# Centring block 0 and multiplying its tokens' scale onto the first layer's sums in an FNet-plus-MLP kernel

## The chip, the cores and the metric

The kernel runs on one core of a Trainium2 chip. The core has a matrix engine (PE, with its weight loads as PEld), a vector engine (DVE), an activation engine (ACT), a general engine (POOL) and a queue processor (SP); SP and POOL issue the transfers here. Every engine works off its own instructions in order and waits for the others by semaphores. The metric is the time of one execution in microseconds (us); runs are given by their median.

## What is computed

```python
x  = A_x                                     # 1 x 2048 x 640, float32
xn = (x - mean(x)) / sqrt(var(x) + 1e-5)     # over the 640 columns
a, b = xn @ dft_hid_re.T, xn @ dft_hid_im.T
y = dft_seq_re @ a - dft_seq_im @ b          # Fourier mixing, real part
h = gelu_tanh(xn @ w1 + b1)                  # w1: 640 x 1536
out = x + y + h @ w2 + b2                    # w2: 1536 x 640
```

## The kernel before, in words

The 2048 tokens are four blocks of 512; a block is four row tiles of 128 tokens by 640 columns. Each float32 operand of a product is split into a high part (ACT copies it to the matrix format, `high`, L186) and a low part (DVE subtracts, `low`, L189), and a product is three matmuls of 512 columns: high by high, high by low, low by high.

The program is written in the order in which every engine is to work; no scheduler moves anything. It begins with block 0. Its four row tiles are loaded (L208) and normalized (L686 to L727: statistics on DVE and ACT, a square root on ACT, three steps of DVE that refine the reciprocal, then subtraction and scaling), while PE runs `NWARM` matmuls on zeros (L666). PE turns the normalized tiles by 20 transposes of 128x128 (L682) into five PSUM banks, from which `XT[j]`, the high and low parts of the five column chunks, are split.

Then come the 12 hidden units of block 0, 128 columns of `w1` each. `hidden(g)` (L308) is 15 matmuls (L320) into one of three banks. `unit` (L332) applies bias and gelu on ACT, from the bank into `ab`; `split_unit` (L343) makes the high and low parts `hs`. `output(g)` (L363) is 15 matmuls (L300 to L302) onto five banks that sum over the units. Step `i` of the loop at L1157 prepares `w1` of unit i+3 and `w2` of unit i+1 (a high part on ACT and a low part on DVE each), issues loads of later weights (three buffers for each of `w1r` and `w2r`), does work of other blocks in `background(i)`, runs `hidden(i+2)`, the gelu and split of that unit, `late(i)`, and `output(i)`.

The other blocks need normalized rows too, for the Fourier part (`xn` in DRAM, written by `put_rows`) and for the hidden units of blocks 1 and 2. Rows of tiles 8 to 11 ("b") and 4 to 7 ("a") are loaded, get statistics (`ln_stats`, L210: two passes over half a row tile and a merge) in steps 0 to 2, a scale (`ln_scale`, L218) and are normalized on DVE (`ln_apply`, L229): "b" in `late(1)`, "a" at the start of step 3. `put_z` (L758) then moves them on the chip into a form `Z`, "b" by eight transfers on SP and eight on POOL, "a" by 16 on POOL. `make_forms` in steps 4, 6 and 7 turns columns of `Z` on DVE (L259) and splits them; `add` (L463) forms differences.

All loads of weights stand on SP's queue in program order. In step 1 the loads of `w1` for unit 7 and of `w2` for unit 5 stand ahead of the eight `z_b` transfers; the load of `w1` for unit 8 stands behind them. A load of `w1` into a buffer waits until the low part of the unit that had it is done.

Of the kernel before, what the change touches and what calls it, by code (L numbers as in the profile page):

```python
# [10 lines left out]
F32 = mybir.dt.float32  # L11
# [4 lines left out]
P = 128  # L16
# [3 lines left out]
NWARM = 19  # L20
NGATE = (7, 10)
# [5 lines left out]
def kernel(  # L27
# [88 lines left out]
    def bank(k):  # L116
        return banks[:, k]
# [15 lines left out]
    ident = early.tile([P, P], F32, name="ident")  # L133
    es_r = ExitStack()
# [41 lines left out]
    def split(hi, lo, src, perm=False):  # L176
# [6 lines left out]
        low(l, s, h)  # L183
# [26 lines left out]
    def ln_stats(c):  # L210
        m = MV
        st = ST[c % 2]
        half = D // 2
        for h in range(2):
            nc.vector.bn_stats(st[:, h, :], xt[c][:, h * half : (h + 1) * half])  # L215
        nc.vector.bn_aggr(m[:, slot[c], 0:2], st.rearrange("p a b -> p (a b)"))  # L216

    def ln_scale(n):  # L218

        m = MV[:, :n]  # L220
        ve, r, t = m[:, :, 2], m[:, :, 3], m[:, :, 4]
        nc.scalar.activation(r, m[:, :, 1], AF.Sqrt, bias=eps[:, 0:1])
        nc.vector.tensor_scalar(ve, m[:, :, 1], EPS, None, op0=ALU.add)
        nc.vector.reciprocal(r, r)
        nc.vector.scalar_tensor_tensor(t, r, -0.5, r, op0=ALU.mult, op1=ALU.mult)
        nc.vector.tensor_tensor(t, t, ve, op=ALU.mult)
        nc.vector.scalar_tensor_tensor(r, t, 1.5, r, op0=ALU.add, op1=ALU.mult)

    def ln_apply(c, eng=nc.vector):  # L229
        m = MV[:, slot[c]]  # L230
        eng.tensor_scalar(xt[c], xt[c], m[:, 0:1], m[:, 3:4], op0=ALU.subtract, op1=ALU.mult)

    def ln_apply_chunked(dst, c, j0=0, j1=ND):

        m = MV[:, slot[c]]
        nc.vector.tensor_scalar(
            chunked(dst)[:, :, j0:j1],
            xt[c].rearrange("p (q c i) -> p q c i", q=Q, i=B)[:, :, j0:j1],
            m[:, 0:1],
            m[:, 3:4],  # L240
            op0=ALU.subtract,
            op1=ALU.mult,
        )
# [43 lines left out]
    def prep_w1(i, n=None):  # L287
        if i < NF:
            W1[i] = slots[1, i]
            split(W1[i][:, 0], W1[i][:, 1], w1r.pop(i if n is None else n).rearrange("p a b -> p (a b)"))  # L290

    def prep_w2(i):
        if i < NF:
            W2[i] = slots[2, i]
            split(W2[i][:, 0], W2[i][:, 1], w2r.pop(i), perm=True)
# [36 lines left out]
    def unit(g, acc, plus=None, a=None):  # L332

        i = g % NF
        if a is None:
            a = mr.tile([P, TB], F32, tag="ab", bufs=2, name=f"ab{g}")
        if plus is not None:
            add(a, plus, acc)
            acc = a
        nc.scalar.activation(a, acc, AF.Gelu_apprx_tanh, bias=b1c[:, i : i + 1])  # L340
        return a
# [9 lines left out]
    FIRST = [(0, 0), (0, 2), (1, 0), (1, 2), (0, 1), (2, 0), (2, 2), (1, 1), (3, 0), (3, 2)]  # L351
    FIRST += [(2, 1), (4, 0), (4, 2), (3, 1), (4, 1)]

# [326 lines left out]
    def transpose_x(c, j0, j1):  # L680
# [5 lines left out]
    last = 1  # L686
    f, m = MV[:, 0], MV[:, last]
    root, step, shift = f[:, 3:4], f[:, 4:5], f[:, 5:6]
    ln_stats(0)
    nc.scalar.activation(root, f[:, 1:2], AF.Sqrt, bias=eps[:, 0:1])  # L690
    scratch = mr.tile([P, 2 * TB], F32, tag="hs", bufs=3, name="scratch")[:, :D]
    nc.scalar.activation(scratch, xt[last], AF.Copy, scale=-1.0 / D, accum_out=m[:, 5:6])
    nc.scalar.activation(
        chunked(xp[:, last]),
        xt[last].rearrange("p (q c i) -> p q c i", q=Q, i=B),
        AF.Identity,
        bias=m[:, 5:6],
    )
    nc.scalar.activation(scratch, xp[:, last], AF.Square, scale=D**-0.5, accum_out=m[:, 1:2])
    nc.vector.reciprocal(root, root)  # L700
    nc.vector.scalar_tensor_tensor(step, root, -0.5, root, op0=ALU.mult, op1=ALU.mult)
    nc.vector.scalar_tensor_tensor(step, f[:, 1:2], EPS, step, op0=ALU.add, op1=ALU.mult)
    for c in (2, 3):
        ln_stats(c)
    others = MV[:, 1:NC]
    v, r, t = others[:, :, 1], others[:, :, 3], others[:, :, 4]
    nc.scalar.activation(r, v, AF.Sqrt, bias=eps[:, 0:1])  # L707
    nc.vector.scalar_tensor_tensor(root, step, 1.5, root, op0=ALU.add, op1=ALU.mult)  # L708
    nc.vector.scalar_tensor_tensor(shift, f[:, 0:1], -1.0, root, op0=ALU.mult, op1=ALU.mult)
    nc.vector.reciprocal(r, r)  # L710
    nc.vector.scalar_tensor_tensor(t, r, -0.5, r, op0=ALU.mult, op1=ALU.mult)
    nc.vector.scalar_tensor_tensor(t, v, EPS, t, op0=ALU.add, op1=ALU.mult)
    nc.vector.scalar_tensor_tensor(r, t, 1.5, r, op0=ALU.add, op1=ALU.mult)
    nc.scalar.activation(  # L714
        chunked(xp[:, 0]),
        xt[0].rearrange("p (q c i) -> p q c i", q=Q, i=B),
        AF.Identity,
        bias=shift,
        scale=root,
    )  # L720
    nc.scalar.activation(xp[:, last], xp[:, last], AF.Copy, scale=m[:, 3:4])
    W1[0], first_w1 = slots[1, 0], w1r.pop(0).rearrange("p a b -> p (a b)")
    nc.scalar.activation(W1[0][:, 0], first_w1, AF.Copy)

    for j0, j1 in ((0, 2), (2, ND)):
        for c in (2, 3):
            ln_apply_chunked(xp[:, c], c, j0, j1)  # L727
# [6 lines left out]
    nc.vector.tensor_tensor(W1[0][:, 1], first_w1, W1[0][:, 0].bitcast(F32), op=ALU.subtract)  # L734
    for j in range(ND):
        split(XT[j][:, 0], XT[j][:, 1], tacc[j])
        if j == 0:
            hidden(0, slice(0, 1))
            transpose_x(3, ND - 1, ND)
    nc.scalar.activation(m[:, 0:1], m[:, 5:6], AF.Copy, scale=-1.0)  # L740
# [8 lines left out]
    acc0 = hidden(0, slice(1, None))  # L749
    prep_w1(1)  # L750
    acc1 = hidden(1)
    prep_w2(0)
    prep_w1(2)
# [19 lines left out]

    def background(i):

        if i == 0:
            for c in range(NC):
                ln_apply(c)
            put_rows(0, row_places)
            ln_stats(8)  # L780
            ln_stats(9)
        if i == 1:
            ln_stats(11)
        if i == 2:
            ln_stats(4)
            ln_stats(5)
# [4 lines left out]
        if i == 6:  # L791
# [3 lines left out]
        if i >= 6:  # L795
            (ua, va), (ub, vb) = ((Z[k][:, :, : 2 * B], Z[k][:, :, 2 * B : 4 * B]) for k in "ab")
        if i == 6:
            add(ub, ub, ua, ALU.subtract)
        if i == 7:
            make_forms("a", "oa0", "va1")  # L800
            open_place(*PLACES[8])
            make_forms("b", "t10", "t11")
        if i == 8:
            add(vb, vb, ub, ALU.subtract)
            turn_x("t20", "b")
            turn_x("t21", "b")
            add(ua, vb, ua, ALU.subtract)
            add(va, va, vb, ALU.subtract)
            load_xo(0)
            for q in range(Q):  # L810
                nc.sync.dma_start(
                    b2c[q * B : (q + 1) * B], b2[q * DQ : (q + 1) * DQ].rearrange("(c i) -> i c", i=B)
                )

    def late(i):

        if i == 0:
            ln_stats(10)
        if i == 1:
            ln_scale(NC)  # L820
            Z["b"] = zo_tile("z_b")
            for c in range(2 * NC, 3 * NC):
                ln_apply(c)
            put_z(Z["b"], A["rows_b"], nc.gpsimd, nc.sync)
            put_rows(2, A["rows_b"])
        if i == 2:
            ln_stats(6)
            ln_stats(7)

    def normalize_a():  # L830
        ln_scale(NC)
        Z["a"] = as_z(row_places)
        for c in range(NC, 2 * NC):
            ln_apply(c)
        put_z(Z["a"], A["rows_a"], nc.gpsimd)

# [250 lines left out]
    def between(p):  # L1087
# [10 lines left out]
        if p == 3:  # L1098
            ln_scale(NC)
# [55 lines left out]
    gelu(0, acc0)  # L1155
    gelu(1, acc1)
    for i in range(NF - 2):  # L1157
        prep_w1(i + 3)
        if i == 3:
            normalize_a()  # L1160
# [3 lines left out]
        prep_w2(i + 1)  # L1164
# [3 lines left out]
        background(i)  # L1168
        acc = hidden(i + 2)
        if i == NF - 3:  # L1170
            more_forms()
        gelu(i + 2, acc)
# [584 lines left out]
```

## Time and profile before

The median of three runs is 851.38 us (851.08 to 852.01).

| | profiled execution before |
|---|---|
| span, first to last instruction | 849.9 us; the page gives no other time of this execution |
| mean granted TensorE clock | 0.998 |
| PE busy | 841.9 us, 99% |
| DVE busy | 686.7 us, 81% |
| ACT busy | 368.6 us, 43% |
| POOL busy | 67.7 us, 8% |
| transfers | 166.53 MB, mean 196 GB/s |

The median of the runs is 1.5 us above this span. A row of the timeline has start, length, engine, line, operation, what is written and read, a count, and in brackets the idle time before it with what ended that. `xab`, `xc`, `as`, `r` and `rt` are the places where the split weights stand, `w1r` and `w2r` the weights as loaded, `banks` is PSUM. "SPq" is SP's queue of issues. A matmul row of 0.39 us has its latency in it; matmuls start 0.23 us apart.

### The profile page before, as it was taken

How to read it: one execution, taken by the hardware profiler on the slowest of the kernel's cores; microseconds unless marked ns; L12 is line 12 of the kernel's file. 1: busy time of each engine (PE TensorE's matmuls, PEld its weight loads, DVE VectorE, ACT ScalarE, POOL GpSimd, SP SyncE). 2: the span in 40 equal slices, each digit the busy share in tenths (PEclk: the TensorE clock that was granted, in tenths of full speed). 3: DMA queues.
4: the chain of work that ended last, by engine and by line, in shares of the span. 5: the costliest groups of instructions: out<-in, count | busy, mean ns of one | idle time of the engine just before them, and what ended most of it. 6: DMA issues, size and time to landing. Idle time of an engine off the chain costs nothing.

```text
span 849.9 us, 10599 instructions
## 1 busy us (share of the span) xinstructions
PE 841.9 (99%) x3711; PEld 696.7 (82%) x3711; DVE 686.7 (81%) x909; ACT 368.6 (43%) x527; POOL 67.7 (8%) x116
## 2 busy tenths in 40 slices
PE   8999999999999999999999999999999999999997
PEld 7888888888888888888888888888888888888886
DVE  7979889767844778979978887889967998885687
ACT  7655666654453555443444344232323433323241
POOL 0440024222301000000000000000000000000002
PEclk9999999999999999999999999999999999999999
DMA  8995667878977897958744679763745799705464
GB/s 230 288 248 158 139 163 250 260 223 305 262 192 199 333 323 138 209 120 193 158 137 107 167 220 283 165 144 99 214 150 156 229 237 234 303 19 180 124 172 108
DMA packets 199141, 166.53 MB, mean 196 GB/s; under 512 B 61648, under 2 KB 170192, under 8 KB 198576
## 3 DMA queue, kind: packets, MB, share of 16 engines
q1 hardware_dynamic: 188320, 140.42, 62.7%
q0 software_dynamic: 7600, 24.91, 8.7%
q10 hardware_dynamic: 3168, 0.52, 0.3%
q8 instruction: 29, 0.48, 0.2%
q14 instruction: 24, 0.20, 0.1%
HBM read 115.75 MB, written 46.14 MB: 190 GB/s over the span
## 4 chain that ended last, share of the span: by engine, by line
PE 98%; DMA 1%; DVE 0%; ACT 0%; SPq 0%; issue 0%; ACTq 0%
PE banks L301 29%; PE banks L302 29%; PE banks L300 29%; PE banks L320 10%; DMA row<-in_A_x_dram 1%; PE banks L682 0%; DVE st L215 0%; ACT xp L714 0%; SPq L208 0%; DVE yo L1722 0%; DVE mv L216 0%; ACT mv L707 0%; DVE mv L708 0%; ACTq L707 0%
## 5 line engine op out<-in xcount | busy, mean ns | idle before, releaser
L186 ACT ACTIVATE as<-r 128x1024 fp32r<-128x1024 f32 x80 | 85.0, 1062 | 171.1 <-PE banks L302 150.4
L300 PE MATMUL banks<-as,xab 128*128 128x512 f32 x407 | 158.3, 389 | 0.0
L302 PE MATMUL banks<-as,xab 128*128 128x512 f32 x407 | 158.3, 389 | 0.0
L301 PE MATMUL banks<-as,xab 128*128 128x512 f32 x407 | 158.3, 389 | 0.0
L189 DVE TENSOR_TENSOR as<-r,as 128x1024 fp32r<-128x1024 f32 x80 | 97.2, 1215 | 38.1 <-ACT as L186 38.0
L301 PEld LDWEIGHTS banks<-as,xab 128*128 128x128 f32 x407 | 76.4, 188 | 15.9
L302 PEld LDWEIGHTS banks<-as,xab 128*128 128x128 f32 x407 | 76.4, 188 | 15.8
L300 PEld LDWEIGHTS banks<-as,xab 128*128 128x128 f32 x407 | 76.4, 188 | 15.8
L300 PE MATMUL banks<-as,xc 128*128 128x512 f32 x224 | 87.1, 389 | 0.0
L301 PE MATMUL banks<-as,xc 128*128 128x512 f32 x224 | 87.1, 389 | 0.0
L302 PE MATMUL banks<-as,xc 128*128 128x512 f32 x224 | 87.1, 389 | 0.0
L186 ACT ACTIVATE as<-rt 128x1024 fp32r<-128x1024 f32 x32 | 34.0, 1063 | 72.5 <-PE banks L302 57.9
L320 PE MATMUL banks<-xt,xab 128*128 128x512 f32 x240 | 56.8, 390 | 0.0
L189 DVE TENSOR_TENSOR hs<-ab,hs 128x512 fp32r<-128x512 f32 x36 | 24.7, 685 | 37.6 <-ACT hs L186 37.6
L320 PEld LDWEIGHTS banks<-xt,xab 128*128 128x128 f32 x240 | 45.0, 188 | 9.4
L301 PEld LDWEIGHTS banks<-as,xc 128*128 128x128 f32 x224 | 42.1, 188 | 8.8
L302 PEld LDWEIGHTS banks<-as,xc 128*128 128x128 f32 x224 | 42.0, 188 | 8.7
L300 PEld LDWEIGHTS banks<-as,xc 128*128 128x128 f32 x224 | 42.1, 188 | 8.7
L1280 POOL DMA_DIRECT2D out_dram<-u x4 | 2.6, 658 | 568.8 <-DVE u L463 568.8
L302 PE MATMUL banks<-hs,xc 128*128 128x512 f32 x120 | 46.7, 389 | 0.0
L300 PE MATMUL banks<-hs,xc 128*128 128x512 f32 x120 | 46.7, 389 | 0.0
L301 PE MATMUL banks<-hs,xc 128*128 128x512 f32 x120 | 46.7, 389 | 0.0
(240 smaller groups left out, 1678.9 us busy)
## 6 DMA issues: line engine op xcount, KB each, us to landing
raw<-in_A_dft_seq_re_dram SPq DMA_DIRECT2D x64, 256.0 KB, 5.4
raw<-in_A_dft_seq_im_dram SPq DMA_DIRECT2D x64, 256.0 KB, 5.1
w1r<-in_B_w_dram SPq DMA_DIRECT2D x144, 80.0 KB, 3.5
wit<-wst POOLq DMA_DIRECT2D x15, 384.0 KB, 4.2
wit<-wst POOLq DMA_DIRECT2D x20, 256.0 KB, 4.5
forms_ab<-xab SPq DMA_DIRECT2D x4, 1280.0 KB, 7.7
xab<-wit SPq DMA_DIRECT2D x13, 384.0 KB, 4.5
row<-xn SPq DMA_DIRECT2D x14, 320.0 KB, 5.3
```

Source lines behind the costliest of these rows:

```text
L186: nc.scalar.activation(h, s, AF.Copy)
L189: nc.vector.tensor_tensor(l, s, h.bitcast(F32), op=ALU.subtract)
L300: nc.tensor.matmul(acc, wh, mh, start=first, stop=False, skip_group_check=goes_on)
L301: nc.tensor.matmul(acc, wh, ml, start=False, stop=False, skip_group_check=goes_on)
L302: nc.tensor.matmul(acc, wl, mh, start=False, stop=last, skip_group_check=goes_on)
L320: nc.tensor.matmul(acc, W1[i][:, a, j * P : (j + 1) * P], XT[j][:, b], start=n == 0, stop=n == len(steps) - 1)
L1280: queues[q % len(queues)].dma_start(rows_of(out, t)[:, :, q * DQ + c0 : q * DQ + c1], src[q * B : (q + 1) * B])
```

## The change

Block 0 is no longer normalized ahead of its products. Its rows are only centred (the mean is subtracted), partly on DVE (`centre`) and partly on ACT (`centre_beside`, with the mean from `mean_beside`); the variance follows later. The scale of each token is computed after the split of `XT`, spread over 128 partitions by four transposes into bank 0, copied to a tile `scale`, and multiplied on DVE onto the sums of every hidden unit of block 0, before its gelu. Rows of block 0 for `xn` are scaled on ACT (`rows_beside`).

```diff
-NWARM = 19
-NGATE = (7, 10)
+NWARM = 14
+NGATE = (6, 9)
...
+        if g < NF:
+            add(a, acc, scale, ALU.mult)
+            acc = a
         nc.scalar.activation(a, acc, AF.Gelu_apprx_tanh, bias=b1c[:, i : i + 1])
...
+    ln_stats(0)
+    centre(0)
+    mean_beside(1)
+    centre_beside(1)
+    spread_beside(1)
+    ln_stats(2)
+    centre(2, 0, 2)
+    mean_beside(3)
+    centre(2, 2, ND)
+    nc.vector.tensor_scalar(MV[:, 3, 0:1], MV[:, 3, 5:6], -1.0, None, op0=ALU.mult)
+    centre_beside(3, 0, 2)
+    centre(3, 2, ND)
     transpose_x(0, 0, ND)
+    transpose_x(1, 0, ND)
     transpose_x(2, 0, 2)
     transpose_x(3, 0, 2)
-    transpose_x(last, 0, ND)
     transpose_x(2, 2, ND)
-    transpose_x(3, 2, ND - 1)
+    transpose_x(3, 2, ND)
     W1[0], first_w1 = slots[1, 0], w1r.pop(0).rearrange("p a b -> p (a b)")
+    nc.vector.tensor_copy(W1[0][:, 0], first_w1)
...
+    acc0 = hidden(0, slice(0, 14))
     prep_w1(1)
-    acc1 = hidden(1)
+    spread_beside(3)
+    ... square root on ACT and four small steps on DVE, for all four tiles
+    prep_w1(2)
     prep_w2(0)
-    prep_w1(2)
+    acc1 = hidden(1, slice(0, 2))
+    hidden(0, slice(14, None))
+    hidden(1, slice(2, 6))
+    for c in range(NC):
+        nc.tensor.transpose(bank(0)[:, c * P : (c + 1) * P], MV[:, c, 3:4].to_broadcast([P, P]), ident)
+    hidden(1, slice(6, None))
+    scale = rows.tile([P, TB], F32, tag="yt", bufs=2, name="scale")
+    nc.scalar.activation(scale, bank(0), AF.Copy)
```

In the loop, the low parts of the weights of a step are put behind that step's multiplication (`rest`, `lows`), the loads of weights behind the gelu, and the normalization of "b" and "a" into the split of the unit of steps 1 and 2: "b" on ACT (`ln_apply_beside`), "a" on DVE and one step sooner. The eight `z_b` transfers of SP now stand ahead of the loads of `w1` for unit 7 and of `w2` for unit 5. The turning of "a" moves from step 6 to 5, later turns move with it.

```diff
     for i in range(NF - 2):
-        prep_w1(i + 3)
-        if i == 3:
-            normalize_a()
+        lows = []
+        prep_w1(i + 3, rest=lows)
...
-        prep_w2(i + 1)
-        if i + 6 < NF + 3:
-            load_w1(i + 6)
-        load_w2(i + 4)
-        background(i)
+        prep_w2(i + 1, lows)
+        rows_beside(i)
+        if i < 4:
+            background(i)
         acc = hidden(i + 2)
...
-        gelu(i + 2, acc)
+        gelu(i + 2, acc, lambda k: beside_split(i, lows) if k else None)
+        if i + 6 < NF + 3:
+            load_w1(i + 6)
+        load_w2(i + 4)
+        if i >= 4:
+            background(i)
         late(i)
         output(i)
```

```python
    def beside_split(i, lows):
        if i == 1:
            ln_scale_table(MV)
            ln_shift()
        for f in lows:
            f()
        if i == 1:
            Z["b"] = zo_tile("z_b")
            for c in range(2 * NC, 3 * NC):
                ln_apply_beside(c)
            put_z(Z["b"], A["rows_b"], nc.gpsimd, nc.sync)
            put_rows(2, A["rows_b"])
        if i == 2:
            ln_scale_table(MVA)
            Z["a"] = as_z(row_places)
            for c in range(NC, 2 * NC):
                ln_apply(c)
            put_z(Z["a"], A["rows_a"], nc.gpsimd)
```

More of the change, by code (lines that the diff above doesn't have):

```diff
@@ L133 @@
     ident = early.tile([P, P], F32, name="ident")
+    MVA = early.tile([P, 4, 6], F32, name="mva")
     es_r = ExitStack()
@@ L182, in split @@
         high(h, s)
-        low(l, s, h)
+        if rest is None:
+            low(l, s, h)
+        else:
+            rest.append(lambda: low(l, s, h))
     def high(h, s):
@@ L699 @@
[L699 to L727, printed above, removed]
+    def centre(c, j0=0, j1=ND):
+        nc.vector.tensor_scalar(
+            chunked(xp[:, c])[:, :, j0:j1],
+            xt[c].rearrange("p (q c i) -> p q c i", q=Q, i=B)[:, :, j0:j1],
+            MV[:, c, 0:1],
+            None,
+            op0=ALU.subtract,
+        )
@@ L783, in background @@
             ln_stats(11)
+            roots(MV)
         if i == 2:
-            ln_stats(4)
-            ln_stats(5)
+            for c in range(NC, 2 * NC):
+                ln_stats(c)
+            roots(MVA)
         if i == 4:
@@ L826, in late @@
         if i == 2:
[L827 to L835, printed above, removed]
+            ln_scale_table(MVA)
+            Z["a"] = as_z(row_places)
+            for c in range(NC, 2 * NC):
+                ln_apply(c)
+            put_z(Z["a"], A["rows_a"], nc.gpsimd)
     XF = {}
@@ L1152, in fourier_step, with second @@
             form(2)
-    gelu(0, acc0)
-    gelu(1, acc1)
+    a0 = unit(0, acc0)
+    a1 = mr.tile([P, TB], F32, tag="ab", bufs=2, name="ab1")
+    def second(k):
+        if k:
+            add(a1, acc1, scale, ALU.mult)
+    split_unit(0, a0, second)
+    nc.scalar.activation(a1, a1, AF.Gelu_apprx_tanh, bias=b1c[:, 1:2])
+    split_unit(1, a1)
     for i in range(NF - 2):
-        prep_w1(i + 3)
-        if i == 3:
-            normalize_a()
+        lows = []
+        prep_w1(i + 3, rest=lows)
         if i == NF - 3:
```

115 lines of the change are left out of this document (67 added, 48 removed).

## The prediction

> **What bounds the kernel now.** I read the page's first part, then the chain of work that ended last, then the timeline at both ends of that chain and in the loop of block 0.
>
> ```profile
> span 849.9 us, 10599 instructions
> PE 841.9 (99%) x3711; PEld 696.7 (82%) x3711; DVE 686.7 (81%) x909; ACT 368.6 (43%) x527; POOL 67.7 (8%) x116
> ```
>
> The chain (start, length, what):
>
> ```profile
> 9.71 2.27 PE banks L682 x19
> ...
> 12.32 10.07 PE banks L320 x44
> ...
> 52.99 3.40 PE banks L320 x15
> ...
> 59.79 3.40 PE banks L320 x15
> ...
> 66.59 3.40 PE banks L320 x15
> ...
> 844.34 0.24 PE banks L302
> 844.61 0.72 DVE yo L1722
> ```
>
> From 12.32 on PE is the chain, at 0.229 us a product (10.07 / 44), in steps of 6.80 us (59.79 - 52.99), until 844.6. PE does not wait there, so the time is the moment at which the first product starts, plus a fixed number of products, plus whatever wait the change puts between them. Only the first 12 us can be shortened.
>
> **The head.** The timeline of the start:
>
> ```profile
> 4.66 0.21 DVE L216 BATCH_NORM_AGGREGATE mv<-st 128x2 f32<-128x12 f32 x1
> 5.10 0.72 ACT L692 ACTIVATE scratch<-row 128x640 f32<-128x640 f32 x1
> 5.95 0.83 ACT L693 ACTIVATE xp<-row,mv 128x640 f32<-128x640 f32 x1
> 6.23 0.89 DVE L215 BATCH_NORM_STATS2 st<-row 128x6 f32<-128x320 f32 x2 [0.46 <-DMA row<-in_A_x_dram]
> 6.81 0.74 ACT L699 ACTIVATE scratch<-xp 128x640 f32<-128x640 f32 x1
> 7.28 0.83 DVE L215 BATCH_NORM_STATS2 st<-row 128x6 f32<-128x320 f32 x2
> 9.60 1.51 DVE L236 TENSOR_SCALAR xp<-row,mv 128x256 f32<-128x256 f32 x4
> 11.03 2.56 ACT L186 ACTIVATE xt<-banks 128x512 fp32r<-128x512 f32 x5
> 11.09 0.82 DVE L734 TENSOR_TENSOR xab<-w1r,xab 128x640 fp32r<-128x640 f32 x1
> 11.73 0.48 PE L320 MATMUL banks<-xt,xab 128*128 128x512 f32 x1
> 11.83 3.07 DVE L189 TENSOR_TENSOR xt<-banks,xt 128x512 fp32r<-128x512 f32 x5
> ```
>
> and two rows of PE's warm-up loads:
>
> ```profile
> 3.80 2.47 PEld L666 LDWEIGHTS banks<-warm 128*128 128x128 f32 x6
> 7.88 0.65 PEld L666 LDWEIGHTS banks<-warm 128*128 128x128 f32 x3
> ```
>
> Before, the first transpose waits for two square roots and their refinement (9.71). After, a tile needs only its mean. Tile 0 is centred right behind 4.87 (0.55 us, by the four parts of L236); tile 1 on ACT, which now begins at the row's landing, some 0.5 sooner than 5.10: done about 6.3; tile 2's statistics stand at 6.23 to 7.36, its centring ends at 8.2; tile 3's mean on ACT runs 7.2 to 8.05 behind tile 1's squares (6.33 to 7.16), its halves are centred by 8.5 (ACT) and 8.8 (DVE). PE itself comes later: warm-up loads run 0.43 apart early and 0.23 at the end, the fourteenth matmul starts beside the fifteenth load, 7.43 (7.88 less two of 0.23), and is issued by 7.66. Then 20 transposes at 0.11 follow without a wait; chunk 0 is whole after the thirteenth, 9.25. ACT's high part takes 0.6 (11.03 to 11.73 with the hand-over): first product at 9.96 instead of 11.73. `w1`'s two first splits, now both on DVE (0.5 + 0.82, 8.8 to 10.1), are ready for the third product, and the low parts of `XT` (0.6 apart from 10.0) keep ahead of the new order of products.
>
> Against that stand a wait of 0.24 for chunk 1 and the four transposes of the scale, 0.44. Their input (squares of tile 3, root, four small steps) is there by 14.6, PE reaches them at 15.0. Hidden unit 2 starts at 9.96 + 30 x 0.229 + 0.24 + 0.44 = 17.5; before it started at 12.32 + 29 x 0.229 = 18.96. Gain 1.46, bounded by 1.2 (each hand-over 0.1 later) and 1.8 (no wait for chunk 1, transposes half hidden). The five warm-up matmuls cost nothing: they ended before PE was wanted.
>
> **The steps.** Durations:
>
> ```profile
> L186 ACT ACTIVATE xab<-w1r 128x640 fp32r<-128x640 f32 x7 | 5.1, 735 | 3.5 <-DMA w1r<-in_B_w_dram 3.5
> ...
> L340 ACT ACT_TABLE_LOAD x3 | 3.8, 1283 | 0.1
> L215 DVE BATCH_NORM_STATS2 st<-r 128x6 f32<-128x320 f32 x8 | 3.5, 475 | 0.0
> ```
>
> DVE gains 12 multiplications that read a bank, 0.6 each back to back (3.07 / 5), 7.2 us; it loses the normalization of block 0 and of "b". ACT takes eight of 640 columns, 0.74 each. Table loads stay as many. None lies on the path by itself: a unit's `hs` is wanted two steps, 13.6 us, after its sums. The low part of the next `w1`, however, now waits for the multiplication, hence for the end of the hidden unit before; it is wanted 3.4 + 0.46 later (third product) and takes 0.6 + 0.82: 2.4 us of slack, if DVE is free. In step 2 it is nearly not: four statistics (1.05 each) stand ahead, and the low part for unit 5 ends at 38.05 against 38.35. No stall, by 0.3.
>
> **Where I expect the loss: the load of `w1` for unit 7.** SP's and POOL's rows, the loop's transfer share, and who used what landed:
>
> ```profile
> 33.64 1.81 SPq L278 DMA_DIRECT2D w1r<-in_B_w_dram  x4
> ...
> 36.04 7.37 SPq L762 DMA_DIRECT2D z_b<-r  x8
> 43.51 6.16 SPq L278 DMA_DIRECT2D w1r<-in_B_w_dram  x4
> 50.18 0.93 SPq L285 DMA_DIRECT2D w2r<-in_B_w_dram  x1
> ```
>
> ```profile
> 35.90 4.36 POOL L762 DMA_DIRECT2D z_b<-r  x8 [8.54 <-ACT xc L186]
> 40.44 2.22 POOL L770 DMA_DIRECT2D xn<-r  x4 [0.19 <-issue]
> 45.43 3.81 POOL L762 DMA_DIRECT2D row<-rt  x7 [2.76 <-DVE rt L231]
> ```
>
> ```profile
> 36.00:48.00 12.00, 12.00 (x54) 9.93 (x54) 11.66 (x28) 8.61 (x12) 9.02 (x17) 1.00 0.96 264
> ```
>
> ```profile
> 54.60 0.72 ACT L186 ACTIVATE as<-w1r 128x640 fp32r<-128x640 f32 x1
> 56.37 0.74 ACT L186 ACTIVATE r<-w2r 128x640 fp32r<-128x640 f32 x1 [1.04 <-DMA w1r<-in_B_w_dram]
> 57.01 0.67 ACT L340 ACTIVATE ab<-banks,b1c 128x512 f32<-128x512 f32 x1
> ```
>
> ```profile
> 58.38 0.69 DVE L189 TENSOR_TENSOR hs<-ab,hs 128x512 fp32r<-128x512 f32 x1 [0.42 <-ACT hs L186]
> ...
> 62.69 1.30 DVE L259 STREAM_TRANSPOSE ztua<-row 128x512 f32<-128x512 f32 x2 [1.05 <-DMA row<-rt]
> ...
> 66.85 1.22 DVE L463 TENSOR_TENSOR z_b<-z_b,row 128x1024 f32<-128x1024 f32 x1
> ```
>
> Transfers are nearly saturated (0.96). The four loads of 33.64, for unit 7, were issued in 1.81 ahead of `z_b`; the four behind it (unit 8) took 6.16 to issue and reached ACT at 54.60, the next `w2r` at 56.37. After, unit 7's stand behind `z_b`. `z_b` itself comes little sooner: unit 2's sums end at 21.1, DVE and ACT walk through four statistics, the root with two table loads and unit 3's gelu until 31.6, four normalizations on ACT end at 34.6, SP issues at 34.8, 1.2 before 36.04. The transfers no longer ahead were worth 2.4 (36.04 - 33.64). So unit 7's `w1` reaches ACT at 54.60 - 3.6 = 51.0, and unit 5's `w2` at 52.8. With the gain, hidden unit 7 is due at 52.99 - 1.46 = 51.5.
>
> Then: high part done 51.8, low part 52.6; unit 7 loses 0.65 and ends at 55.55. `w2`'s split, the gelu of unit 6 and its split follow in ACT's order; from `w2` to DVE's `hs` 2.0 (56.37 to 58.38), another 0.6, then the forms of "b", 4.16 (62.69 to 66.85), all ahead of unit 7's multiplication on DVE: 59.5. The low part for unit 8 ends at 60.9; its third product was due at 55.55 + 3.4 + 0.46 = 59.4: 1.5 more. DVE now carries 2.67 a step (0.6 + 2 x 0.735 + 0.6) plus 4.16 and, in step 5, the difference of 1.13: it does not catch up. The multiplication of unit 8 comes at 67.75, the low part for unit 9 at 69.15 against 67.7: 1.5 more. Step 6 has only 2.6 of forms; there the delay ends. Stall 0.65 + 1.5 + 1.5 = 3.6.
>
> Bounds: if those loads issue and land as those of 33.64 did, they are there before 48, stall 0; if only the 1.2 counts, `w2` comes at 55.2, and all of the extra 2.4 is stall: 6.0. I take 3.6, the middle, as SP's rows behind `z_b` are the nearest.
>
> Sum: -1.46 + 3.6 = +2.1 on the span of 849.9, 852.0. The median of the runs, 851.38, stands 1.5 above that span; the same added gives 853.5.
>
> **The rivals.** The granted clock first, for the second of them:
>
> ```profile
> core 0: 849.9 us, clock 0.998
> ```
>
> (1) The loads land in time and nothing stalls. For it: `z_b` now meets an emptier SP queue, and DVE alone, at 6.83 of 6.80 in step 4, just holds. Against it: the four loads behind `z_b` took 11 us from their first issue (43.51) to ACT (54.60), while POOL's queue moved its half of `z_b`, then `xn`, then "a". "In time" means `w2` by 49.2, 3.6 sooner than 52.8. Time: 851.38 - 1.46 = 849.9.
>
> (2) The clock is not up. Warm-ups start 0.43 apart, later 0.23 (rows above); with 14 only two run at the full pace. If the change of pace came after the last warm-up, eight to sixteen products at 0.2 more cost 1.6 to 3.2: 851.5 to 853.1, or more with the stall. Against it: the clock of the whole execution is 0.998, and the pace, still 0.43 at 6.2 (3.80 + 2.47), has changed before the fourteenth. The Trainium skill ("TensorE: Matmul & The Clock Gate", "What's actually happening") says that the gate opens after a free-running window of about 3.4 us of work and that the count of slow matmuls varies by run; the trace agrees that there is one change of pace, and no run shown has it later than 7.4. By that rule alone the sum would be what this rival gives in an unlucky run.
>
> (3) Transfers are fine, but DVE falls behind in step 2 (0.3 of slack): stalls of 0.3 to 2, 850.2 to 851.9.
>
> (4) More is saved at the head than 1.8, as parts of the transposes overlap: below 849.5.
>
> **How the numbers follow.** A measurement tells about 0.2%, 1.7 us, from no change: faster is below 849.68, slower above 853.08. The stall has 0.55 (852.2 to 855.9; of it 0.45 above 853.08, 0.10 below); rival 1 has 0.34 (849.5 to 850.3; 0.15 faster, 0.19 same); rival 2 0.05 (0.03 slower, 0.02 same); rival 3 0.03, same; rival 4 0.03, faster. Faster 0.18, same 0.34, slower 0.48. The range runs from 849.6 to 855.9; the stall case alone from 852.2 to 855.9.
>
> **What would show it.** Right: first product near 10.0, unit 2 at 17.5; ACT waiting for `w1r` near 51 and for `w2r` near 53; PE idle before units 7, 8 and 9, in all 3 to 4 us, and none after 75. Wrong: unit 7 starting at 51.5 with no idle PE in the chain; or products at 0.43 behind 10 us; or a PE that waits at 15 for the scale or at 38 for unit 5.

## The result, and the profile after

The kernel after the change takes 856.26 us by the median of six executions (855.09 to 857.87); the kernel before, run beside it, 851.37 us (851.08 to 852.01). The ratio is 1.0055, 95% interval 1.0042 to 1.0068. The prediction was 853.5 us with a range of 849.6 to 855.9: the sign and the place of the loss were right, the size was too small by 2.8 us, and the median lies 0.4 us above the range.

The first lines of the page after:

```profile
span 853.2 us, 10601 instructions
...
PE 842.6 (99%) x3710; PEld 695.6 (82%) x3710; DVE 688.6 (81%) x905; ACT 375.7 (44%) x538; POOL 67.6 (8%) x116
```

This execution took 855.09 us, so it is the quickest of the six. The chain of work that ended last, from the head to 80 us (start, length, what):

```profile
7.50 2.19 PE banks L696 x20
9.69 5.24 PE banks L331 x21
14.93 0.44 PE banks L772 x4
15.36 5.47 PE banks L331 x24
...
24.23 3.40 PE banks L331 x15
...
44.63 3.41 PE banks L331 x15
...
51.00 5.41 DMA w1r<-in_B_w_dram
56.48 3.95 DMA w1r<-in_B_w_dram
...
68.47 0.68 DVE ab L477
69.16 0.74 DVE as L193
69.94 3.24 PE banks L331 x13
...
76.59 3.40 PE banks L331 x15
```

The head is as forecast: the 20 transposes follow the warm-ups without a gap, PE does not wait at the four transposes of the scale (14.93), and hidden unit 3 starts at 24.23. That is 6.80 behind unit 2 at 17.43, which in the kernel before started at 18.96: a gain of 1.53. Then, between 51 and 70 us, PE leaves the chain for the first time since the head, to a DMA of `w1r` and to DVE. The timeline there shows who waited:

```profile
51.56 0.74 ACT L190 ACTIVATE xab<-w1r 128x640 fp32r<-128x640 f32 x1 [7.92 <-DMA w1r<-in_B_w_dram]
...
52.35 4.12 PE L331 MATMUL banks<-xt,xab 128*128 128x512 f32 x15 [0.92 <-ACT xab L190]
...
53.63 0.74 ACT L190 ACTIVATE xc<-w2r 128x640 fp32r<-128x640 f32 x1 [1.33 <-DMA w2r<-in_B_w_dram]
...
59.71 0.72 ACT L190 ACTIVATE as<-w1r 128x640 fp32r<-128x640 f32 x1
...
60.44 0.68 DVE L477 TENSOR_TENSOR ab<-banks,scale 128x512 f32<-128x512 f32 x1
...
60.48 0.73 PE L331 MATMUL banks<-xt,as 128*128 128x512 f32 x2 [0.60 <-ACT as L190]
61.04 0.81 DVE L193 TENSOR_TENSOR as<-w1r,as 128x640 fp32r<-128x640 f32 x1
...
61.91 3.25 PE L331 MATMUL banks<-xt,as 128*128 128x512 f32 x13 [0.70 <-DVE as L193]
```

Unit 7 (52.35) waits for the high part of its `w1`, for which ACT stood still 7.92 us. Unit 8 waits twice: at 60.48 for its high part, which ACT copies (59.71) behind the high parts of the forms of "b", and at 61.91 for its low part, behind the multiplication and the forms on DVE. Unit 9 (69.94) waits for its low part alone. Taken as what the starts of two products stood apart beyond 0.227 us, the idle PE is 1.59 before and in unit 7, 1.86 in unit 8 (0.88 of it for the high part) and 1.20 in unit 9: 4.65 us in all, and nothing more until the end. -1.53 + 4.65 = +3.1, and the spans differ by 853.2 - 849.9 = 3.3.

SP's queue in the same stretch:

```profile
34.47 6.18 SPq L784 DMA_DIRECT2D z_b<-r  x8
40.75 7.63 SPq L289 DMA_DIRECT2D w1r<-in_B_w_dram  x4
48.48 1.48 SPq L296 DMA_DIRECT2D w2r<-in_B_w_dram  x1
```

The four loads for unit 7 stand behind `z_b` and take 7.63 us to issue; before, ahead of `z_b`, they took 1.81.

### The profile page after: what moved, and what is told of

Read it like the earlier page. It is cut to its first block, busy times and chain, and to the rows that moved or that the text cites. A ratio compares the mean times of both kernels' runs of the same rounds, so it can differ in the third digit from the quotient of the medians.

```text
span 853.2 us, 10601 instructions
## 1 busy us (share of the span) xinstructions
PE 842.6 (99%) x3710; PEld 695.6 (82%) x3710; DVE 688.6 (81%) x905; ACT 375.7 (44%) x538; POOL 67.6 (8%) x116
## 4 chain that ended last, share of the span: by engine, by line
PE 97%; DMA 1%; DVE 1%; issue 0%; SPq 0%; ACT 0%; DVEq 0%
PE banks L313 29%; PE banks L312 29%; PE banks L311 29%; PE banks L331 9%; DMA w1r<-in_B_w_dram 1%; PE banks L680 1%; PE banks L696 0%; DVE as L193 0%; DVE ab L477 0%; ACT xab L190 0%; SPq L296 0%; SPq L289 0%; DVE xab L193 0%; DVE r L193 0%; DVE ztva L270 0%
```

## The experiments

All times are medians, each with the kernel before run beside it (851.5 to 852.0 us).

**Both loads ahead of `z_b`** (loads_first, and once more as loads_again). In `beside_split(1)`, the loop leaving these two out in step 1:

```diff
+            load_w1(i + 6)
+            load_w2(i + 4)
             put_z(Z["b"], A["rows_b"], nc.gpsimd, nc.sync)
```

> The kernel after the change, with the loads of w1 for unit 7 and of w2 for unit 5 issued ahead of the z_b transfers, everything else in place. If the late load is the whole cause of the 4.6 us in which PE stands idle between 51 and 70 us, that idle time goes and only the gain of the head is left: 851.4 - 1.5 = 849.9 us by the median (849.5 to 850.4). If DVE, with the multiplications, is what cannot keep up in steps 4 to 6, the waits before units 8 and 9 (0.9 and 1.1 us in the profiled execution) stay: about 852 us, and the profile shows the low part of unit 8's w1 still ending near 62 us.

> The same kernel as loads_first (both loads ahead of the z_b transfers) once more, for a second trace. Eight of its twelve executions took 851.0 to 853.0 us at a granted clock of 0.998 to 1.0, four took 856.9 to 858.0 us at 0.994 to 0.996. If there is a chance event in this kernel, about one execution in three is again near 857 us, and where the profiled one is, its trace shows either products 0.43 apart (the clock) or a wait for a load between 45 and 70 us.

Measured: 852.66 us (twelve executions, 851.02 to 858.01; ratio 1.0025, 1.0008 to 1.0042) and 853.20 us (nine, 850.96 to 855.73). The waits before units 7 and 8 are gone in both traces. So the late loads were the larger cause: with them gone the median falls by 3.1 to 3.6 us. But neither theory gives the spread, and both profiled executions are quick ones (851.02 and 851.94). In the timelines of loads_first (first fence) and loads_again (second), one wait of DVE is new to the reading:

```profile
32.91 1.82 SPq L289 DMA_DIRECT2D w1r<-in_B_w_dram  x4
...
35.33 7.46 SPq L784 DMA_DIRECT2D z_b<-r  x8
...
58.89 1.30 DVE L270 STREAM_TRANSPOSE ztua<-row 128x512 f32<-128x512 f32 x2 [0.75 <-DMA row<-rt]
```

```profile
59.80 1.30 DVE L270 STREAM_TRANSPOSE ztua<-row 128x512 f32<-128x512 f32 x2 [1.74 <-DMA row<-rt]
...
66.57 3.24 PE L331 MATMUL banks<-xt,as 128*128 128x512 f32 x13 [0.99 <-DVE as L193]
```

DVE stands still until the last `z_a` transfer has landed, because the forms of "a" are now turned in step 5. Behind them on DVE stand the multiplication of unit 8 and the low part of `w1` for unit 9. In the kernel after itself this wait does not show, since DVE came to the forms only at 63.19, held up by the late loads.

**`w2` alone ahead** (w2_first): only `load_w2(5)` is moved ahead of `z_b`.

> The kernel after the change, with the load of w2 for unit 5 alone issued ahead of the z_b transfers; the four loads of w1 for unit 7 stay behind them. The wait before unit 7 (about 1.6 us with its broken start) stays under every theory. If the waits of units 8 and 9 come from w2 of unit 5, which holds up the split of unit 6 and with it DVE's queue, they shrink to about 0 to 1.5 us: 852 to 853.5 us. If they come from w1 of unit 7 itself, because ACT stands at it in order, nothing moves: about 855 to 856 us.

Measured: 854.65 us (854.00 to 855.90). In its trace the idle PE is 2.87 in unit 7, 0.42 in unit 8, 1.19 in unit 9. The wait of unit 8 has shrunk, as one of the theories has it, but unit 7 waited longer here, and a PE that is later itself may find unit 8's weights ready. This run does not settle how much is owed to `w2`.

**Without the multiplications** (no_mult): the late loads stay.

```diff
-        if g < NF:
-            add(a, acc, scale, ALU.mult)
-            acc = a
         nc.scalar.activation(a, acc, AF.Gelu_apprx_tanh, bias=b1c[:, i : i + 1])
```

> The kernel after the change without its twelve multiplications by the tokens' scale (the gelu of block 0 reads the sums unscaled, so block 0's hidden values lack their scale); the late loads stay. By the late load the wait before unit 7 stays at about 1.6 us, and those of units 8 and 9 lose at most 0.7 us each, since the low parts of w1 still stand behind the forms in DVE's queue: idle PE 3 to 4 us in place of 4.6, 854 to 855.5 us. If the multiplications are the cause, all idle time goes: about 850 us.

The multiplication of unit 1, which stands ahead of the loop, goes too. Measured: 855.33 us (854.87 to 857.15). The multiplications are not the main cause: without them 3.9 of the 4.9 us of loss remain. The trace has 2.8 us of idle PE before unit 7, nearly none before units 8 and 9, and something that no theory had: behind the wait six products lie 0.43 apart. Two stretches of its windows (the stretch and its length; PE, PEld, DVE, ACT, POOL busy with their counts; then the granted clock, the share of the DMA engines, GB/s):

```profile
51.00:55.00 4.00, 1.38 (x6) 0.64 (x4) 0.59 (x1) 0.74 (x1) 2.39 (x5) 1.00 1.09 250
55.00:59.00 4.00, 3.87 (x11) 2.95 (x11) 2.91 (x5) 2.45 (x4) 0.55 (x1) 0.57 1.11 241
```

The granted clock is 0.57 as a mean over the 4 us behind the wait, and eleven products start where 18 would at 0.227 us.

**The kernel before with the loads behind `z_b`** (before_behind): step 1 leaves the two loads out of their old place, and nothing else is changed.

```diff
+        if i == 1:
+            load_w1(i + 6)
+            load_w2(i + 4)
         output(i)
```

> The kernel before, with the loads of w1 for unit 7 and of w2 for unit 5 put behind the z_b transfers and nothing else changed. If the place of these loads is the cause by itself, w1 of unit 7 reaches ACT near 54 to 55 us, when unit 7 is due at 53.0: PE waits 2 to 6 us, 853.5 to 857 us. If it takes the multiplications or the earlier forms too, the kernel before has slack for it: at most 1 us, 851.4 to 852.4 us.

Measured: 853.58 us (853.08 to 856.52; ratio 1.0028, 1.0017 to 1.0039). The order on SP alone costs the kernel before 2.1 us, with neither multiplications nor earlier forms (in the profiled execution, of 854.88 us, PE stands idle 1.99 us in unit 7 and 0.95 in unit 8):

```profile
35.51 6.91 SPq L762 DMA_DIRECT2D z_b<-r  x8
...
42.52 6.19 SPq L278 DMA_DIRECT2D w1r<-in_B_w_dram  x4
...
53.72 0.74 ACT L186 ACTIVATE xab<-w1r 128x640 fp32r<-128x640 f32 x1 [8.55 <-DMA w1r<-in_B_w_dram]
...
54.51 4.09 PE L320 MATMUL banks<-xt,xab 128*128 128x512 f32 x15 [1.31 <-ACT xab L186]
```

The loads take 6.19 us to issue in place of 1.81, and reach ACT 11.2 us after the first issue.

**Other numbers of warm-ups**, on loads_first (loads_19, loads_10): `NWARM = 19` with `NGATE = (7, 10)`, and `NWARM = 10`.

> loads_first with the warm-ups of the kernel before (19 matmuls, their gates at 7 and 10, in place of 14, 6 and 9). If the executions near 857 us come from too few warm-ups (the clock not yet up when the products begin, or lost again before them), they are gone here; the price is five matmuls of 0.23 us ahead of the transposes, at most 1.1 us: 851.5 to 853 us, highest under 854. If they come from loads that land late now and then, about a third of the executions stay near 857 us.

> loads_first with 10 warm-up matmuls, four fewer. They end near 6.3 us, about 1.2 us before the first transpose can start, so nothing of the head is gained by it. If warm-ups are what decides the slow executions, most executions here show products 0.43 apart behind 10 us (8 to 16 of them, 1.6 to 3.2 us): 853.5 to 857 us or more. If they do not, nothing moves: 851 to 853 us with the same third near 857 us.

Measured: 856.11 us with 19 (852.33 to 858.81), 853.03 us with 10 (851.44 to 858.02). Executions near 857 us are there with more warm-ups and with fewer, and no slow product stands at the head of either trace. Both traces are of quick executions, though, and five of eight executions with 19 lie above 855.3, against four of twelve and one of nine with 14 and two of ten with 10: whether the number of warm-ups changes how often this happens is not shown. The first product starts at 10.01 with 19 and at 9.61 with 10, against 9.70 and 9.73 with 14. The trace with 10 shows the largest wait for `z_a` so far:

```profile
61.16 1.30 DVE L270 STREAM_TRANSPOSE ztua<-row 128x512 f32<-128x512 f32 x2 [3.18 <-DMA row<-rt]
...
67.92 2.35 PE L331 MATMUL banks<-xt,as 128*128 128x512 f32 x9 [1.84 <-DVE as L193]
```

**The forms in the steps of the kernel before**, with the loads first (loads_forms) and with the loads late (forms_later): `put_rows(1)`, the forms of "a" and the first difference go from step 5 back to step 6, those behind them one step further.

> loads_first with the forms of the Fourier part turned in the steps of the kernel before (a in step 6, not 5; the rest behind it). loads_first has 0.28 us of idle PE left at 65 us, where the low part of w1 for unit 9 stands behind the forms of a. If the spread of 851.0 to 853.0 us comes from DVE's queue there, the quick executions move together near 850.8 us; if it comes from the head or from the loads, the spread stays.

> The kernel after the change with the late loads left in place and the forms of the Fourier part turned in the steps of the kernel before (a in step 6). If the late loads and the early forms are two causes, the waits before units 7 and 8 stay (1.6 and 1.9 us in the profiled execution), the one before unit 9 (1.1 us) goes, and about 1.5 us comes at 79 and 103 us as in loads_forms: 855 to 857 us, with no gain in the median but a narrower spread. If the early forms are the whole cause, about 852 us.

Measured: 853.12 us (852.65 to 853.84, eleven executions; ratio 1.0018, 1.0010 to 1.0027) and 857.49 us (856.53 to 858.35). With the loads first and the forms late, the executions near 857 us are gone; the spread is 1.2 us. The median is no better, as 0.36 and 1.75 us of idle PE come at 79 and from 103 us on; both waits name DVE, which now has four forms in step 7 and three differences in step 8. With the loads late, all of it adds up: in this trace `w1` of unit 7 reached ACT at 54.06 and PE waited 3.4 us.

**The kernel after once more** (after_again):

> The kernel after the change once more, for a trace of an execution that is not its quickest (855.1 us in the profile at hand, median 856.3). If what varies is the landing of z_a and the loads behind z_b, the difference to 855.1 us stands in the idle PE before units 7, 8 and 9 (more than 4.6 us in all), with an unchanged head and nothing behind 75 us; where PE stands still for more than about 2 us, products 0.43 apart may follow. If it is the head or the end, the idle time there is 4.6 us again.

Measured: 856.92 us (856.48 to 857.73); its profiled execution took 856.89. Both the head and the loads vary: the first product starts at 10.41 (9.61 in the first trace), and PE loses 5.7 us between 51 and 72. Its loads, and two stretches of its windows:

```profile
41.75 7.44 SPq L289 DMA_DIRECT2D w1r<-in_B_w_dram  x4
...
53.36 0.74 ACT L190 ACTIVATE xab<-w1r 128x640 fp32r<-128x640 f32 x1 [8.68 <-DMA w1r<-in_B_w_dram]
```

```profile
51.00:55.00 4.00, 1.96 (x8) 0.98 (x6) 0.83 (x1) 0.74 (x1) 3.35 (x7) 1.00 1.03 220
55.00:59.00 4.00, 3.99 (x11) 3.16 (x12) 2.30 (x4) 2.11 (x4) 0.00 (x0) 0.57 1.10 251
```

2.08 us of idle PE (2.60 with the gaps between the first products of unit 7), then eight products at 0.43 for another 1.6, then 0.3 before unit 8 and 1.2 before unit 9. At the head, all 14 warm-ups lie 0.43 or more apart (in the first trace the last three intervals are shorter), so that the transposes start at 7.93 in place of 7.34, and tile 3 landed 0.7 us late for ACT.

**`z_a` sooner** (rows_last, rows_sp, rows_sp_late), each on loads_first. The four transfers that write the rows of "b" go: behind `z_a` on POOL; to SP behind its `z_b`; to SP behind the loads of step 2.

```diff
-            put_rows(2, A["rows_b"])
...
+        if i == 2:
+            put_rows(2, A["rows_b"], nc.sync)
```

> loads_first (both loads ahead of the z_b transfers) with the four transfers that write the rows of b to DRAM moved behind the 16 z_a transfers on POOL's queue. In the three traces of loads_first and loads_10 the idle PE at 65 us (0.28, 1.25 and 2.6 us) follows DVE's wait for z_a at the first turning of a (0.75, 1.74, 3.18 us). If that wait is the cause of the spread, z_a lands about 2 us sooner here, the wait is gone or below 1 us, and the executions lie at 850.5 to 852 us, under the kernel before (851.5). If the transfers are simply saturated and something else is late in its place, the spread to 857 us stays.

> loads_first with the four transfers that write the rows of b to DRAM on SP's queue behind its z_b transfers, in place of POOL's queue ahead of z_a. In rows_last z_a landed at 56.3 us (58.8 in loads_first) and DVE did not wait for it, but the rows of b were read until 60.3 us, and w2 of unit 6, which is split into the place that they stand in, came late: that idle PE was a new wait. Here z_a keeps the gain and the rows are read by about 50 us. If DVE's wait for z_a is what spreads the executions of loads_first, all lie at 850.4 to 852 us with no idle PE of more than 0.5 us between 45 and 75 us. If SP's loads of w1 for units 8 and 9, now behind four more transfers, come late instead, PE waits there and the time is 852 to 855 us.

> loads_first with the four transfers that write the rows of b on SP's queue behind the loads of step 2 (w1 of unit 8, w2 of unit 6). In rows_last those loads were issued by 44.0 us and z_a landed at 56.3 us; the rows would follow from about 44 us and be read by about 52 us, ahead of the split of w2 of unit 6 into their place near 55 us. If the late landing of z_a is the cause of the spread, DVE does not wait for it, idle PE between 45 and 75 us is below 0.5 us, and all executions lie at 850.3 to 851.5 us, under the kernel before. If transfers between 36 and 60 us are too many in any order, one of z_a, w1 of unit 9 or w2 of unit 6 is late again: 852 to 857 us.

Measured: 857.66 us (857.23 to 859.33), 857.13 us (853.81 to 857.73), and 852.64 us (851.70 to 853.48, eleven executions; ratio 1.0013, 1.0004 to 1.0022). In rows_last `z_a` was there in time, but the rows of "b" were read until 60.3 us and the place they stand in is where `w2` of unit 6 is split to: some 4.7 us of idle PE and slow products again. The trace of rows_last shows one thing more. The four loads of `w1` for unit 8, directly behind `z_b` on SP as in loads_first, take 2.06 us to issue in place of 6.92 and have landed 5.6 us after the first issue in place of 10.6; the one edit between the two kernels is that the writes of the rows of "b" come later. In rows_sp the four writes stood ahead of `w1` of unit 8, which came 2.2 us late for ACT. Only in the third is nothing late by much. Its timeline:

```profile
56.56 0.74 ACT L190 ACTIVATE r<-w2r 128x640 fp32r<-128x640 f32 x1 [1.40 <-DMA row<-rt]
...
59.22 1.30 DVE L270 STREAM_TRANSPOSE ztua<-row 128x512 f32<-128x512 f32 x2
```

DVE no longer waits for `z_a`, the idle PE of unit 9 is 0.73 us, no execution is above 853.5 and no granted clock is below 0.998. ACT still waits 1.40 us for the place of the rows of "b" (the row names another transfer; the last write of these rows landed at 56.4). Here and in loads_forms, the two kernels in which DVE does not wait for `z_a` and no load is much late, the executions near 857 us are gone: these runs point to the landing of `z_a` as the source of the spread. The median stays 0.13% above the kernel before.

**Half of the forms behind the low parts** (forms_split with the loads first, forms_split_after with the loads late): one form of "a" and the difference go behind the low parts of step 6.

> loads_first with one of the three forms of a that step 5 turns, and the difference of 1.13 us, put behind the low parts of step 6; no transfer is moved. DVE then has 2.6 us of forms in place of 5.1 between z_a's landing and the multiplication of unit 8, so that z_a can land as late as about 61 us without a wait of PE. If the place of the forms is the cause of the spread, no execution lies above 853 us, the idle PE at 65 us is below 0.3 us, and the median is 850.3 to 851.2 us, under the kernel before. If transfers come late wherever DVE's work stands, executions near 857 us stay, with idle PE before another unit.

> The kernel after the change with the same part of a's forms put behind the low parts of step 6, the late loads of w1 for unit 7 and w2 for unit 5 left in place. If the late loads are the larger cause, the waits before units 7 and 8 stay (3.0 us in the profile of the kernel after, 3.0 with its slow products in the second one) and the last one, before unit 9, goes: 854 to 856 us. If the forms are the larger cause, below 853.5 us.

Measured: 854.86 us (852.96 to 856.21) and 856.84 us (855.85 to 857.24). The wait of unit 9 is gone in forms_split, and the same 2.3 us of idle PE stand before units 10 and 11. DVE waited 2.78 us for `z_a` in this trace and had no spare time later to make it good. My expectation that moving work on DVE would do was wrong: the idle time only moves. With the loads late the wait before unit 7 was 3.0 us, and the median is that of the kernel after.

**Less work on DVE** (loads_no_mult: loads_first without the multiplications; subs_pool, split_subs_pool: loads_first and forms_split with four differences of 128x1024 on POOL).

```diff
-            add(ub, ub, ua, ALU.subtract)
+            nc.gpsimd.tensor_tensor(ub, ub, ua, op=ALU.subtract)
...
```

> loads_first without the twelve multiplications by the tokens' scale (block 0's hidden values lack their scale). If DVE has too little spare time for a wait on z_a because of the multiplications (0.6 us a step, and the low parts no longer wait for the sums), the executions lie together at 849.5 to 851.5 us with idle PE under 0.5 us. If late transfers decide by themselves, the spread stays: median near 853 us, some at 857 us.

> loads_first with the four differences of the Fourier part (128x1024, 1.22 us each on DVE in steps 5, 7 and 8) on POOL, which stands idle there. If DVE's time is what is short, 1.2 us of it comes free ahead of the multiplication of unit 8: executions that had 0.3 to 1.4 us of idle PE have none, those with 2.6 us keep about 1.4: median 850.3 to 851.5 us, highest under 854. If POOL's differences take so long that DVE waits for them, or if transfers decide, 852 to 857 us.

> forms_split (both loads ahead of z_b, one form of a behind the low parts of step 6) with the same four differences on POOL. forms_split had no idle PE before unit 9 and 2.3 us before units 10 and 11. If DVE's time is what is short, those 2.3 us go: all executions at 850 to 851.5 us, under the kernel before. If transfers decide, the median stays near 854 to 855 us.

Measured: 852.14 us (850.28 to 857.35, twelve executions), 860.12 us (859.56 to 860.56), 858.38 us (856.74 to 860.21). Without the multiplications the quick executions come down to 850.3 us, but four of twelve are at 855 to 857 us; the profiled one is of these and shows what they are:

```profile
62.48 1.31 DVE L270 STREAM_TRANSPOSE ztua<-row 128x512 f32<-128x512 f32 x2 [2.94 <-DMA row<-rt]
...
68.64 1.65 PE L331 MATMUL banks<-xt,as 128*128 128x512 f32 x3 [1.24 <-DVE as L193]
```

```profile
68.00:72.00 4.00, 3.36 (x9) 2.71 (x10) 3.90 (x7) 1.90 (x4) 0.00 (x0) 0.57 0.71 168
```

`z_a` landed 2.9 us late, PE stood still 1.27 and 1.41 us, and the clock fell to 0.57: some 4.3 us together. The executions of loads_first near 857 us were not profiled; their granted clock (0.994 to 0.996 against 0.998 to 1.0) is near that of this one (0.996), so slow products are likely in them too; what was late in them is not shown. The differences on POOL made DVE slower, not freer; the timeline of subs_pool:

```profile
63.53 2.41 POOL L833 TENSOR_TENSOR z_b<-z_b,row 128x1024 f32<-128x1024 f32 x1 [6.50 <-DMA w1r<-in_B_w_dram]
64.42 2.07 DVE L193 TENSOR_TENSOR xab<-ztua,xab 128x512 fp32r<-128x512 f32 x1
```

A low part that takes 0.69 us alone takes 2.07 beside it. The Trainium skill ("SBUF — State Buffer", "Who interferes with whom") says that a DVE operation with two inputs in SBUF contends with a GpSimd operation that reads SBUF, over a shared port pair that is an exclusive lock; this trace agrees, with 2.07 to 2.91 for 0.69.

Over the kernels with the loads first, the multiplications in place and the forms of "a" whole in step 5 on DVE (rows_last, late for another reason, left out), the start of DVE's first turning of "a" and the idle PE before unit 9 (slow products left out) go together:

| | first turning at | idle PE, unit 9 | this execution |
|---|---|---|---|
| loads_first | 58.89 | 0.29 | 851.0 |
| rows_sp_late | 59.22 | 0.73 | 852.4 |
| loads_again | 59.80 | 1.26 | 851.9 |
| loads_19 | 60.24 | 1.37 | 852.3 |
| rows_sp | 60.80 | 2.00 | 853.8 |
| loads_10 | 61.16 | 2.71 | 853.2 |

From 58.9 on, a microsecond at the turning is about a microsecond of PE.

## Why the prediction was wrong, point by point

**PE as the chain, and the head: right.** First product 9.61 (said: 9.96), unit 2 at 17.43 (17.5), gain 1.53 (1.46, bounds 1.2 to 1.8), no wait for the scale or in step 2 (w2_first has one there, 0.42 us at 32.10 in unit 4). The first product came 0.35 sooner than said and unit 2 only 0.07, so that two small misses cancel in the gain. What the bounds left out is that the head varies: in after_again the first product came at 10.41, as the pace of the warm-ups changed later and tile 3 landed later. In the 20 traces the warm-ups change pace from the seventh on at the earliest, and in after_again not before the last of 14: rival 2, a change behind the last warm-up, was nearer than "no run shown has it later than 7.4" let it seem. "The five warm-up matmuls cost nothing" was near: 19 of them put the first product 0.3 later in the one trace.

**The loss and its place: right.** The load of `w1` for unit 7 behind `z_b`, waits before units 7, 8 and 9, none after 75. loads_first takes the first two waits away, before_behind brings them into the kernel before.

**The size of the stall: the step that failed.** "Stall 0.65 + 1.5 + 1.5 = 3.6", with `w1` at ACT at 51.0 and `w2` at 52.8. In the first trace they are there at 51.56 and 53.63, and the stall is 1.59 + 1.86 + 1.20 = 4.65. That was the quickest execution. In the other traces of the kernel after and its versions with both loads late, `w1` reaches ACT at 53.36 (after_again), 53.64 (no_mult), 54.06 (forms_later) and 54.35 (forms_split_after).

The term that was mis-sized is "The transfers no longer ahead were worth 2.4". From the first issue of `z_b` on SP to `w1` at ACT, the kernel before took 18.56 us (36.04 to 54.60). The first trace took 17.09 (34.47 to 51.56), after_again 17.87, and no_mult, forms_split_after and forms_later 18.94 to 19.45: 1.5, 0.7 and nothing of the 2.4. My own rows had the better figure: "34.8" for the first `z_b`, 7.5 to the first load behind it (36.04 to 43.51) and the 11 us from there to ACT that I named against rival 1 give about 53.3. Besides, I took one trace as the middle of what varies: from first issue to ACT the loads took 10.8 us in the first trace, 11.6 in after_again and 12.75 in forms_later. In unit 8 I had the low part on DVE alone; 0.88 of its 1.86 us is for the high part on ACT.

**A term that was missing: the clock.** I had the clock as a rival at the head only. PE stood still for 2.1 us in the loop of after_again, and the granted clock over the next 4 us was 0.57: another 1.6 us. The Trainium skill page that the prediction names for the head also speaks of gaps above some 3 us inside a kernel ("TensorE: Matmul & The Clock Gate", "Why this matters for your kernels"); here 2.1 and 2.8 us were enough in two traces, while 3.4 us in forms_later and 3.0 in forms_split_after brought no slow product. What tells these apart is where the gap lies. In all 20 traces the granted clock changes only at the ends of equal steps of 3.41 us, which lie differently in every execution, and between head and end it is 1.00 or 0.50 in each. With the idle PE summed by step (as in the section on the result), nine steps hold 2.10 us or more, and the clock is 0.50 in the step behind each of them; no step with 2.08 or less is followed by one at 0.50. Those on both sides of that line, and some more:

| trace and step | idle PE in it | granted clock in the next |
|---|---|---|
| after, 50.83 to 54.24 | 1.59 | 1.00 |
| forms_split_after, 50.53 to 53.95 | 1.81 | 1.00 |
| forms_later, 53.49 to 56.90 | 1.87 | 1.00 |
| rows_sp, 65.21 to 68.62 | 2.00 | 1.00 |
| forms_later, 50.08 to 53.49 | 2.08 | 1.00 |
| rows_last, 64.24 to 67.66 | 2.10 | 0.50 |
| loads_no_mult, 64.86 to 68.28 | 2.42 | 0.50 |
| after_again, 52.14 to 55.55 | 2.53 | 0.50 |
| no_mult, 51.63 to 55.04 | 2.95 | 0.50 |

The 3.4 us of forms_later fell into two steps, and neither had enough. The clock is not all of the slow executions: of the six of the result the one at 857.32 us has a mean clock of 1.0.

**Rival 1 could not have come out as told.** "The loads land in time and nothing stalls: 849.9" has its condition met in loads_first, and the median there is 852.7 to 853.2. I had the forms of "a" in step 5 as work of DVE, and did not ask when their rows land: a wait of DVE of 0.75 to 3.2 us, with the low part of unit 9 behind it. It is the third part of the change, and I gave it no price. The row at 62.69 that I took as the price of the forms of "b" is the turning of "a" in the kernel before, and it showed 1.05 us of just this wait.

**The base.** I added the 1.5 us between the median and the profiled span. In 106 executions of the kernel before, time and span of the same execution are 1.95 apart by the median, with a median span of 849.6: the profiled one (849.9) was somewhat slow itself. 0.4 us of the miss is this.

So 856.26 - 853.5 = 2.8 is made of 0.4 from the base, 1.05 of stall in the quickest execution less 0.07 of head, 0.2 that no step accounts for, and 1.2 by which the median execution is slower than that one; after_again shows where such time can go, to later loads, a lower clock and a later head. The range's upper end (stall 6.0, from the same single trace) had none of these.

Open: how the loss divides between `w1` and `w2` (w2_first did not tell), and whether the loads for unit 7 are late for `z_b` ahead of them or for the writes of the rows of "b" in flight beside them. By rows_last the second may be the larger part, but no run has the late loads with these writes moved. No version that keeps the multiplications beats the kernel before: the best, rows_sp_late and loads_forms, are at 1.0013 and 1.0018 of it, so that what the head gains is spent again on the way.

## What to carry to other kernels

When an edit puts a load behind bulk transfers on its queue, the price is not the issue time in front of it but its whole flight under saturated transfers, and that varies by microseconds from one trace to the next: give it a range from issue to use, and look which other transfers are in flight then. Add what the clock takes when PE stands still for most of a step of 3.41 us; gaps of 2 to 3.4 us cost 1.6 us more or nothing here, by where they fell. When work is moved to the step in which its input lands, ask what stands behind it on that engine, in order; where the engine has no spare time, each microsecond of late input comes out at the bound. And if the gain is 1.5 us at the head, check that every transfer in the next 60 us is still as early as before.

## What the runs showed of the hardware that I had not expected

- The granted clock goes by steps of 3.41 us: behind each of the nine steps with 2.10 to 3.19 us of idle PE it is 0.50 for a step, behind the others (at most 2.08) 1.00. With one such step, six to eight products lie 0.43 apart, 1.5 to 1.6 us more.
- Four loads of `w1r` take 1.81 us to issue on SP ahead of `z_b` and 4.3 to 7.8 behind it, yet 2.02 and 2.06 behind it in rows_sp_late and rows_last, where POOL's queue goes straight on to `z_a`. Against loads_first (6.92), rows_last moves only the writes of the rows of "b": what the other queue moves sets SP's issue time here.
- Four 128x1024 differences on POOL (2.4 to 2.7 us each) stretch DVE's low parts beside them from 0.69 to between 2.07 and 2.91 us; the median is 7.5 us above that of loads_first.
